# Decay matrices of the later chunks: VectorE's scans replaced by ScalarE's exponentials of cumulated logarithms, with GpSimd setting the upper triangle to zero

## The chip, the cores and the metric

One core of a Trainium2 chip runs the whole kernel. The time is the device time of one launch in microseconds (us). TensorE (PE, with its weight loads as PEld), VectorE (DVE), ScalarE (ACT), GpSimd (POOL) and SyncE (SP, which here only issues DMAs) each run their own instruction stream in order and wait for each other by semaphores.

## The reference

The first half is a state-space layer over 4 sequences, 8 heads and 768 tokens. It yields `y` per token and head; the second half is a mixture of four two-layer experts over the 3072 tokens.

```python
for c in range(nc):
    la = log_a[:, :, sl]                       # log of the decays a, clipped to 1e-6..1
    cum = np.cumsum(la, axis=-1)
    L = np.exp(cum[:, :, :, None] - cum[:, :, None, :])
    L = L * causal                             # i >= j
    M = np.einsum('bhin,bhjn->bhij', Cc, Bc) * L
    y_intra = np.einsum('bhij,bhjd->bhid', M, xc)
    y_inter = np.einsum('bhin,bhnd->bhid', Cc, state) * np.exp(cum)[:, :, :, None]
    y[:, :, sl] = y_intra + y_inter
    state = decay_full[:, :, None, None] * state + np.sum(Bx, axis=2)
...
for e in range(E):                             # x: y with the heads side by side
    out += p[:, e:e + 1] * (np.maximum(x @ w1[e], 0.0) @ w2[e])
```

`L[i, j]` is the product of the decays of the tokens j+1 to i. So a row of it can be made by a running product from a 1 on the diagonal, or as the exponential of a difference of two running sums of logarithms, with zeros where i < j.

## The kernel before

The kernel cuts each sequence into chunks of 128 tokens (not the reference's 32): 24 chunks, each with 8 heads. Chunk c belongs to sequence c mod 4, so chunks 0 to 3 are the first ones of their sequences and need no state. The chunks are grouped into five blocks of 4, 4, 4, 6 and 6, and inside a block into pairs. A block of tokens is then multiplied with the experts' weights (TensorE products at line 871, by schemes that save multiplications and pay with sums of blocks on VectorE and GpSimd: lines 898, 962, 981, 1200).

For each chunk the state-space half does this:

- `fetch` (line 741) loads the tokens `xb`, a copy `ab` of the chunk's decays to all 128 partitions (line 439, 512 KB, from the DRAM tensor `acut_d`, in which the first decay of each chunk is 0), and from the fifth chunk on `ah` (line 445, from `ac_d`, the uncut decays).
- `decays` (line 755) makes `LT`, the transposed decay matrices of the 8 heads: from chunk 3 on two VectorE scans of 128x512 (line 495), each over four heads, with the identity as addend: a running product that restarts at every diagonal. `LT` has one buffer for a pair of chunks. GpSimd's `fade` (line 505) takes the last column of `LT` for the state. For chunks from the fifth on, VectorE also scans `ah` into `dec` (line 777, 128x128), and GpSimd multiplies it into `cts` (line 780). ScalarE makes the masked `ctm` (line 471).
- `scores` (line 784): TensorE multiplies C and B for a pair (line 478) into four PSUM banks; four VectorE instructions (line 795, 128x512) multiply these with `LT` into `MT`, which has two buffers for pairs.
- `outputs` (line 803): TensorE multiplies `MT` (line 511) and the state (line 817); ScalarE copies the results out of PSUM (lines 832, 521). `carry` (line 839) updates the state on VectorE.

In the expert half the products of a unit are chained through PSUM: ScalarE copies a bank out (`snap`, line 880, and line 1148) or loads a bank with a saved partial sum (`seed`, line 885), and VectorE gates a bank with relu and probability (`gated`, line 906). TensorE's next product of the same bank waits for these copies.

The first 13 us (lines 525 to 697, chunks 0 and 1 and the start of 2) are written out by hand. All that follows is ordered at build time by `Plan` (line 81): TensorE's order is a fixed list (`line`), and for each other engine `run` (line 187) simulates the times with given durations and takes, whenever an engine is free, the ready instruction with the earliest latest permissible start (`w.latest`, line 140). Two rules of it matter here. `hold` (lines 138 and 139) tightens that start of an instruction to a given time after the product that it reads. And a free VectorE, in the first 25 us alone (`NEAR`, `FIRST`, lines 237 and 241), may leave a ready instruction and wait for a much more urgent one that is ready within 0.3 us. What comes out is a fixed instruction order on each engine and on SP's DMA queue. Where a pair's decays, scores and outputs are put into the list is said in `PAIRS_AT` (line 48).

Buffers are "homes" of a kind: 33 of kind V (128x512), 28 of kind W (weights), 8 PSUM banks, 2 `ab`, 2 `MT`, 1 `LT`.

Of the kernel before, what the change touches and what calls it, by code (L numbers as in the profile page):

```python
# [8 lines left out]
FP32 = mybir.dt.float32  # L9
AF = mybir.ActivationFunctionType  # L10
ALU = mybir.AluOpType
# [18 lines left out]
AFTER = 1  # L30
HOLD = 6.0
NEAR, WORTH, FIRST = .3, 1.0, 25.0
WAIT = .15
# [47 lines left out]
class Plan:  # L81
# [12 lines left out]
    def add(self, on, fn, reads=(), writes=(), part=(), lag=None, due=None, reuse=None, two=False,  # L94
            port=True, after=None, kb=0, hold=0.0, pieces=1):
        w = Work(on, fn, (.16 if "PE" in on else .09) if lag is None else lag)
        w.hold = hold
        w.two, w.port, w.after, w.kb, w.pieces = two, port, after, kb, pieces
        w.due, w.reuse = due, reuse
        w.ready = 0.0  # L100
        for v in reads:
            w.needs.update(v.writers)
            w.ready = max(w.ready, getattr(v, "ready", 0.0))
            v.readers.append(w)
        for v in writes:
            w.needs.update(v.writers)
            w.needs.update(v.readers)
            v.writers, v.readers = [w], []
        for v in part:
            w.needs.update(v.readers)  # L110
            v.writers = v.writers + [w]
        w.needs.discard(w)
        for v in dict.fromkeys([*reads, *writes, *part]):
            w.touched.append(v)
            v.left += 1
        for n in w.needs:
            n.feeds.append(w)
        w.number = len(self.all)
        self.all.append(w)
        return w  # L120
# [66 lines left out]
    def run(self, line, at, begin):  # L187
# [19 lines left out]
        while todo:  # L207
# [4 lines left out]
            for w in waiting[e]:  # L212
# [23 lines left out]
                else:  # L236
                    if e == "DVE" and when <= now + NEAR and now < FIRST and (near is None or rank < near[0]):
                        near = rank, when
# [103 lines left out]
def kernel(  # L342
# [33 lines left out]
    def real(c):  # L376
        return c % NSEQ * NC + c // NSEQ
# [14 lines left out]
    acut_d = tc.dram_tile([NCH, NH, P], FP32, name="acut_d")  # L392
    ac_d = tc.dram_tile([NCH, NH, P], FP32, name="ac_d")
    p_d = tc.dram_tile([E, NCH, P], FP32, name="p_d")
# [9 lines left out]
    def some(n, shape, name, pool=const):  # L404
        return [pool.tile(shape, FP32, name=f"{name}{i}") for i in range(n)]

    homes = {
        "V": some(NV, [P, 2, FB], "v"),
        "W": some(NW, [P, 2 * FB], "w"),
# [3 lines left out]
        "ah": some(3, [HN, P], "ah"),  # L413
        "LT": some(1, [P, 2, NH, P], "LT"),
        "MT": some(2, [P, 2, NH, P + N], "MT"),
# [5 lines left out]
        "gate": some(3, [P, max(b.n for b in blocks), P], "gate"),  # L421
        "Y": some(12, [P, FB], "Y"),
    }
    st = {c: {} for c in range(NCH)}
    one = nc.const_aps.tensor(1.0, [P, 1])
# [11 lines left out]

    def load_decays(c, ab):
        nc.sync.dma_start(
            out=ab, in_=acut_d[real(c)].rearrange("h s -> (h s)").partition_broadcast(P))  # L440

    def load_heads(c, ah):
        src = ac_d[real(c)].unsqueeze(1).to_broadcast([NH, N, P])
        for there, here, n in turned(c):
            nc.sync.dma_start(out=ah[here:here + n], in_=src[there // N:(there + n) // N])
# [47 lines left out]
    def scan(LT, src, lo):  # L493
# [4 lines left out]
            op0=ALU.mult, op1=ALU.add)  # L498

    def fade(c, MT, xb, LT):  # L500
        b = xb[:, OB:OB + HN].rearrange("p (h n) -> p h n", h=NH)
# [14 lines left out]
    def keep_state(c, A, y):  # L516
# [13 lines left out]
    pc = const.tile([P, NCH, E], FP32)  # L530
    a_sb, a_cut = (homes["V"][-4][:NCH * NH // 2, i].rearrange("p (r s) -> p r s", r=2) for i in range(2))
    nc.gpsimd.memset(aq0, 0.0)
# [6 lines left out]
        out=aq1.rearrange("(q r) c t s -> q r c (t s)", q=NQ)[:, 0], in_=a_rows[:, 1:SPREAD])  # L539
    warm = const.tile([P, 1], FP32)  # L540
    nc.scalar.mul(warm, one, one)

# [90 lines left out]

    LT, MT = ([homes[k][0][:, c] for c in range(2)] for k in ("LT", "MT"))
    ctm = homes["ctm"]
# [60 lines left out]
    nc.sync.dma_start(out=p_d.rearrange("e c s -> c e s"), in_=p_sb)  # L696
    store_decays(nc.sync, ac_d, a_sb)

# [38 lines left out]
    for c in range(2):  # L737
        st[c]["A"] = plan.taken("A", c, now)
    g0 = gates[0, 0] = plan.taken("gate", 0, now)

    def fetch(c):
# [5 lines left out]
        if c >= NSEQ:  # L747
            s["ah"] = value("ah")
            dma(lambda e: load_heads(c, s["ah"].t), len(turned(c)), 64,
                part=[s["ah"]])  # L750
        if "ab" not in s and c >= SPREAD:
            s["ab"] = value("ab")
            dma(lambda e: load_decays(c, s["ab"].t), 1, 512, part=[s["ab"]])

    def decays(c):
        s = st[c]
        j = c % 2
        for k in ("LT", "MT") if not j else ():
            s[k] = st[c + 1][k] = value(k)
        for part in range(2):  # L760
            if c < SPREAD:
                dve(1.2, lambda e, part=part: scan_quarters(
                    c, s["LT"].t[:, j], [b.t for b in s["a"]], part), reads=s["a"][2 * part:2 * part + 2],
                    part=[s["LT"]])
            else:
                half = NH * P // 2
                dve(1.15, lambda e, lo=half * part: scan(
                    s["LT"].t[:, j], s["ab"].t[:, lo:lo + half], place(c, lo // P) * P), two=True, reads=[s["ab"]], part=[s["LT"]])
        if c < NCH - NSEQ:
            plan.add({"POOL": .5 if place(c, 0) else .4}, lambda e: fade(c, s["MT"].t[:, j], s["xb"].t, s["LT"].t[:, j]),  # L770
                     reads=[s["xb"], s["LT"]], part=[s["MT"]])
        if "ctm" not in s:
            s["ctm"] = value("ctm")
            act(.62, lambda e: mask(c, s["ctm"].t, s["xb"].t), reads=[s["xb"]], writes=[s["ctm"]])
        if c >= NSEQ:
            s["dec"], s["cts"] = value("dec"), value("cts")
            dve(D256, lambda e: nc.vector.tensor_tensor_scan(
                out=s["dec"].t, data0=s["ah"].t, data1=zeros, initial=1.0,
                op0=ALU.mult, op1=ALU.add), two=True, reads=[s["ah"]], writes=[s["dec"]])
            plan.add({"POOL": .72}, lambda e: nc.gpsimd.tensor_mul(  # L780
# [3 lines left out]
    def scores(cs):  # L784
# [6 lines left out]
        for r in (3, 2, 0, 1):  # L791
            def fn(e, r=r):
                g = gs_[r].t.rearrange("p (c t s) -> p c t s", c=2, t=NT)[:, :len(cs)]
                js, h = slice(cs[0] % 2, cs[0] % 2 + len(cs)), quarter(cs[0], r)
                nc.vector.tensor_mul(s["MT"].t[:, js, h, 0:P], g, s["LT"].t[:, js, h])  # L795

            dve(D512 if len(cs) > 1 else D256, fn, reads=[gs_[r], s["LT"]], part=[s["MT"]], hold=HOLD)

# [104 lines left out]
    def gated(x, g, n, sign=1):  # L903
# [5 lines left out]
                [P, JJ, FB]), op0=ALU.max if sign > 0 else ALU.min, op1=ALU.mult),  # L909
            reads=[x, g], writes=[h], reuse=x, two=x.kind != "bank")  # L910
        return h
# [383 lines left out]
    twos = [(fb, fb + 1) for fb in range(0, AHEAD * EPB, 2)]  # L1295

    st[2]["a"] = [value("bank", fills=False) for _ in range(NQ)]
    fetch(3)
# [11 lines left out]
    scores([2, 3])  # L1310
    line.extend(firsts[SCORED:8])
    outputs([2, 3])
    ones = [(two, {1: begun[two][2]}) for two in twos]
    line.extend([*firsts[8:], *second(0, ones[:SOON], [(1, 2)])])
    for c in range(4):
# [148 lines left out]
```

## Time and profile before

| | us |
|---|---|
| median of 3 runs | 623.88 (623.32 to 623.90) |
| span of the profiled execution, first to last instruction | 620.9 |
| what lies around the span, if that execution took the median | 3.0 |
| PE / PEld busy | 615.4 / 526.0 |
| DVE busy | 533.5 |
| ACT busy | 275.5 |
| POOL busy | 179.1 |
| DVE scans into `LT` of 128x512 (line 495), 42 | 54.5 |
| DVE scans into `dec` (line 777), 20 | 11.7 |

The profile gives no total time of the profiled execution besides its span. Shares of busy time are averages over the whole span. A view by stretches of time gives the busy time of each engine in each stretch, with the number of instructions in brackets, then the granted TensorE clock, the DMA engines' busy share and GB/s. In the timeline, an entry has its start, how long it and the following like instructions took, the engine, line and operation, and in square brackets the idle time of the engine before it and what ended it. Matmul ends are modelled, so on TensorE the distances of the starts are the better measure.

### The profile page before, as it was taken

The numbers are of one execution on the slowest core, as the hardware profiler recorded it, in microseconds if no ns is written. First come the engines' busy times: TensorE is split into PE (matmuls) and PEld (weight loads), VectorE is DVE, ScalarE is ACT, GpSimd is POOL, SyncE is SP. The second block draws the span as 40 slices with busy tenths as digits, with TensorE's granted clock in tenths as the row PEclk, the third lists the DMA queues.
The fourth block names the chain that finished last, engine by engine and source line by source line (L and its number), as shares of the span: only waits on it lengthen the run. The fifth ranks groups of instructions, "written<-read, shape, count | busy, mean of one in ns | idle before, by whom it ended". The sixth has DMA issues, their size and how long they took to land.

```text
span 620.9 us, 10264 instructions
## 1 busy us (share of the span) xinstructions
PE 615.4 (99%) x3427; PEld 526.0 (85%) x3427; DVE 533.5 (86%) x882; ACT 275.5 (44%) x582; POOL 179.1 (29%) x205
## 2 busy tenths in 40 slices
PE   9999999999999999999999999999999999999997
PEld 5788888888888888888888888888888888888886
DVE  7999999999868779879799999959787977869684
ACT  5453373523356334235534336446443334555441
POOL 5006586544326676362542110300000000000010
PEclk9999999999999999999999999999999999999999
DMA  7997779773799779399998929635231339643001
GB/s 254 331 346 231 239 247 307 240 237 103 226 359 303 264 233 306 84 298 322 293 338 280 333 66 307 177 117 177 60 106 57 86 66 309 209 138 111 1 1 51
DMA packets 112627, 127.44 MB, mean 205 GB/s; under 512 B 28980, under 2 KB 78144, under 8 KB 112576
## 3 DMA queue, kind: packets, MB, share of 16 engines
q1 hardware_dynamic: 112420, 126.74, 63.8%
q8 instruction: 27, 0.44, 0.3%
q14 instruction: 24, 0.20, 0.1%
q10 hardware_dynamic: 156, 0.06, 0.0%
HBM read 101.87 MB, written 24.89 MB: 204 GB/s over the span
## 4 chain that ended last, share of the span: by engine, by line
PE 97%; DVE 1%; ACT 1%; issue 0%; DVEq 0%
PE bank L871 91%; PE bank L511 2%; PE bank L478 2%; PE bank L649 1%; PE bank L817 1%; PE bank L625 0%; DVE v L906 0%; DVE w L962 0%; DVE LT L495 0%; DVE MT L795 0%; ACT ctm L471 0%; DVE v L898 0%; PE bank L1269 0%; PE bank L617 0%; ACT A L521 0%
## 5 line engine op out<-in xcount | busy, mean ns | idle before, releaser
L871 PE MATMUL bank<-v,w 128*128 128x256 f32 x1816 | 429.5, 380 | 0.7 <-ACT v L880 0.3
L871 PEld LDWEIGHTS bank<-v,w 128*128 128x128 f32 x1816 | 342.7, 190 | 53.8 <-issue 4.0
L871 PE MATMUL bank<-Y,w 128*128 128x256 f32 x824 | 210.6, 379 | 0.0
L898 DVE TENSOR_TENSOR v<-v,v 128x512 f32<-128x512 f32 x258 | 188.9, 764 | 16.4 <-ACT v L880 15.2
L871 PEld LDWEIGHTS bank<-Y,w 128*128 128x128 f32 x824 | 156.3, 190 | 21.9 <-issue 0.6
L906 DVE SCALAR_TENSOR_TENSOR v<-bank,gate 128x512 f32<-128x512 f32 x172 | 116.2, 683 | 32.6 <-PE bank L871 27.7
L885 ACT COPY bank<-v 128x512 f32<-128x512 f32 (+1 forms) x201 | 112.8, 573 | 67.8 <-DVE v L898 37.1
L962 POOL TENSOR_TENSOR w<-w,w 128x256 f32<-128x256 f32 x100 | 95.1, 973 | 60.2 <-PE bank L871 23.1
L1148 ACT COPY v<-bank 128x512 f32<-128x512 f32 x106 | 62.2, 587 | 110.6 <-PE bank L871 109.7
L880 ACT COPY v<-bank 128x512 f32<-128x512 f32 x112 | 65.5, 586 | 95.7 <-PE bank L871 92.3
L898 POOL TENSOR_TENSOR v<-v,v 128x512 f32<-128x512 f32 x22 | 30.3, 1382 | 261.8 <-DVE v L898 157.6
L495 DVE TENSOR_TENSOR_SCAN LT<-ab,ident 128x512 f32<-128x512 f32 x42 | 54.5, 1317 | 0.4 <-DMA ab<-acut_d 0.4
L898 DVE TENSOR_TENSOR v<-bank,v 128x512 f32<-128x512 f32 x40 | 27.5, 687 | 7.9 <-PE bank L871 7.5
L1200 DVE TENSOR_TENSOR v<-v,v 128x256 f32<-128x256 f32 x56 | 24.6, 476 | 6.8 <-ACT v L1148 6.7
L780 POOL TENSOR_TENSOR cts<-ctm,dec 128x256 f32<-128x256 f32 x20 | 18.4, 929 | 33.3 <-ACT ctm L471 17.0
L795 DVE TENSOR_TENSOR MT<-bank,LT 128x512 f32<-128x512 f32 x44 | 27.2, 679 | 0.5
L1151 ACT COPY v<-bank 128x256 f32<-128x256 f32 x23 | 8.6, 374 | 40.2 <-PE bank L871 40.1
L505 POOL TENSOR_TENSOR MT<-xb,LT 128x64 f32<-128x64 f32 (+1 forms) x28 | 14.6, 529 | 36.9 <-DVE LT L495 29.7
L962 POOL TENSOR_TENSOR w<-w 128x256 f32<-128x256 f32 x13 | 14.6, 1125 | 20.1 <-PE bank L871 12.1
L1047 DVE TENSOR_TENSOR bank<-bank,v 128x512 f32<-128x512 f32 x24 | 16.5, 692 | 3.0 <-PE bank L871 2.8
L471 ACT ACTIVATE ctm<-xb,tmask 128x128 f32<-128x128 f32 x48 | 16.1, 397 | 0.0
L962 DVE TENSOR_TENSOR w<-w,w 128x256 f32<-128x256 f32 x38 | 16.0, 459 | 0.0
(72 smaller groups left out, 202.5 us busy)
## 6 DMA issues: line engine op xcount, KB each, us to landing
w<-w_d SPq DMA_DIRECT2D x138, 256.0 KB
w<-in_w_dram SPq DMA_DIRECT2D x126, 256.0 KB
w_d<-w SPq DMA_DIRECT2D x82, 256.0 KB
ab<-acut_d SPq DMA_DIRECT2D x21, 512.0 KB
w<-in_w_dram SPq DMA_DIRECT2D x42, 128.0 KB
gate<-p_d SPq DMA_DIRECT2D x10, 384.0 KB
xb<-in_xbc_dram SPq DMA_DIRECT2D x17, 192.0 KB
gate<-p_d SPq DMA_DIRECT2D x11, 256.0 KB
```

What stands on the lines that cost most here:

```text
L495: nc.vector.tensor_tensor_scan(out=LT.rearrange("p h s -> p (h s)")[:, lo:lo + w], data0=src, data1=ident.rearrange("p h s -> p (h s)")[:, ...
L780: plan.add({"POOL": .72}, lambda e: nc.gpsimd.tensor_mul(s["cts"].t, s["ctm"].t, s["dec"].t.unsqueeze(1).to_broadcast([HN, NT, P])), reads ...
L795: nc.vector.tensor_mul(s["MT"].t[:, js, h, 0:P], g, s["LT"].t[:, js, h])
L871: nc.tensor.matmul(out=o, lhsT=w[:, j], rhs=x if half is None else x[:, j], start=(start and j == 0), stop=(j == 1), skip_group_check=True)
L880: act(.5, lambda e: nc.scalar.copy(out=flat(v), in_=bank.t), reads=[bank], writes=[v])
L885: act(.54 if to - lo > FB else .32, lambda e: nc.scalar.copy(out=bank.t[:, lo:to], in_=flat(v)[:, lo:to]), reads=[v], writes=[bank])
L898: plan.add(engines, lambda e: (on(e).tensor_add if sign > 0 else on(e).tensor_sub)(flat(v), whole(x), whole(y)), reads=[x, y], writes=[v], ...
L906: dve(D512, lambda e: nc.vector.scalar_tensor_tensor(out=h.t, in0=whole(x).rearrange("p (j m) -> p j m", j=JJ), scalar=0.0, in1=g.t[:, 2 * ...
L962: plan.add({"POOL": .72} if due else B256, lambda e, r=r, x=x, y=y, sign=sign: (on(e).tensor_add if sign > 0 else on(e).tensor_sub)(view(r ...
L1047: dve(D512, lambda e: nc.vector.tensor_sub(b5.t, b5.t, flat(t)), reads=[t], writes=[b5])
L1148: act(.5, lambda e: nc.scalar.copy(out=flat(v), in_=bank.t), reads=[bank], writes=[v])
L1200: plan.add(engines, lambda e: (on(e).tensor_add if sign > 0 else on(e).tensor_sub)(o[1](), x[1](), y[1]()), reads=[v for v in vs if v is n ...
```

## The change

Chunks 0 to 3 keep their scans, into a tile `LT0` whose four quarters then become V homes (29 other V tiles, so again 33, and `LT` is no longer a buffer of its own). For the chunks from the fifth on:

- Once, early in the plan: ScalarE takes the logarithm of the clipped decays (128 columns of two rows, on 96 partitions), VectorE sums them up in two scans, SP stores the sums to the DRAM tensor `cum_d`, TensorE transposes them (two transposes), and ScalarE stores them negated as `neg`, one column for each chunk and head. The store of the uncut decays to `ac_d` at the end of the hand-written part goes.
- For each chunk: `ab` and `ah` are loaded from `cum_d`. Eight ScalarE exponentials of 128x128 (one for each head, the bias a column of `neg`) write straight into `MT`, two GpSimd selects of 128x512 set the part above the diagonal to zero in place, `fade` reads `MT`, one ScalarE exponential of 128x128 makes `dec`, and line 795's four products read and write `MT`.
- The planner may let ScalarE too, at any time, wait for a more urgent instruction that is ready within `NEAR`, now 0.4 us; and `gated` instructions that read a bank get a `hold` of 2 us.
- ScalarE's small warming multiplication becomes an explicit load of a table set with logarithm and exponential.

```diff
-HOLD = 6.0
-NEAR, WORTH, FIRST = .3, 1.0, 25.0
+HOLD, FREE = 6.0, 2.0
+NEAR, WORTH, FIRST = .4, 1.0, 25.0
...
+        w.needs.update(behind)
...
-                    if e == "DVE" and when <= now + NEAR and now < FIRST and (near is None or rank < near[0]):
+                    if when <= now + NEAR and (e == "ACT" or e == "DVE" and now < FIRST) and (
+                            near is None or rank < near[0]):
...
-        "V": some(NV, [P, 2, FB], "v"),
+        "V": some(NV - 4, [P, 2, FB], "v"),
...
-        "LT": some(1, [P, 2, NH, P], "LT"),
...
+        "cum": some(2, [NCH * NH // 2, 2, P], "cum"),
+        "neg": some(1, [P, 2, NCH * NH // 2], "neg"),
+        "dram": [None],
     }
+    LT0 = const.tile([P, 2, NH, P], FP32, name="LT0")
+    homes["V"][:0] = [
+        LT0[:, j, h:h + NQ].rearrange("p (a h) s -> p a (h s)", a=2)
+        for j in range(2) for h in range(0, NH, NQ)]
...
+        src = acut_d if c < NSEQ else cum_d
         nc.sync.dma_start(
-            out=ab, in_=acut_d[real(c)].rearrange("h s -> (h s)").partition_broadcast(P))
+            out=ab, in_=src[real(c)].rearrange("h s -> (h s)").partition_broadcast(P))
 
     def load_heads(c, ah):
-        src = ac_d[real(c)].unsqueeze(1).to_broadcast([NH, N, P])
+        src = cum_d[real(c)].unsqueeze(1).to_broadcast([NH, N, P])
...
+    def decay(c, MT, ab, neg, h):
+
+        nc.scalar.activation(
+            out=MT[:, place(c, h), 0:P], in_=ab[:, h * P:h * P + P], func=AF.Exp,
+            bias=neg[:, h % NT, NQ * real(c) + h // NT:NQ * real(c) + h // NT + 1])
+
+    def causal(MT, h, n):
+        nc.gpsimd.affine_select(
+            out=MT[:, h:h + n, 0:P], in_=MT[:, h:h + n, 0:P], compare_op=ALU.is_ge, fill=0.0,
+            base=0, pattern=[[0, n], [1, P]], channel_multiplier=-1)
...
-    warm = const.tile([P, 1], FP32)
-    nc.scalar.mul(warm, one, one)
+    nc.scalar.preload_act_table_set("natural_log_exp_and_others")
...
-    store_decays(nc.sync, ac_d, a_sb)
...
-        for k in ("LT", "MT") if not j else ():
-            s[k] = st[c + 1][k] = value(k)
-        for part in range(2):
-            if c < SPREAD:
-                dve(1.2, lambda e, part=part: scan_quarters(
-                    c, s["LT"].t[:, j], [b.t for b in s["a"]], part), reads=s["a"][2 * part:2 * part + 2],
-                    part=[s["LT"]])
-            else:
-                half = NH * P // 2
-                dve(1.15, lambda e, lo=half * part: scan(
-                    s["LT"].t[:, j], s["ab"].t[:, lo:lo + half], place(c, lo // P) * P), two=True, reads=[s["ab"]], part=[s["LT"]])
-        if c < NCH - NSEQ:
-            plan.add({"POOL": .5 if place(c, 0) else .4}, lambda e: fade(c, s["MT"].t[:, j], s["xb"].t, s["LT"].t[:, j]),
-                     reads=[s["xb"], s["LT"]], part=[s["MT"]])
+        if not j:
+            s["MT"] = st[c + 1]["MT"] = value("MT")
+            s["made"] = st[c + 1]["made"] = []
+        if c < NSEQ:
+            for part in range(2):
+                if c < SPREAD:
+                    dve(1.2, lambda e, part=part: scan_quarters(
+                        c, LT0[:, j], [b.t for b in s["a"]], part),
+                        reads=s["a"][2 * part:2 * part + 2], part=LTv[2 * j:2 * j + 2])
+                else:
+                    half = NH * P // 2
+                    dve(1.15, lambda e, lo=half * part: scan(
+                        LT0[:, j], s["ab"].t[:, lo:lo + half], lo), two=True,
+                        reads=[s["ab"]], part=LTv[2 * j:2 * j + 2])
+            plan.add({"POOL": .4}, lambda e: fade(
+                c, s["MT"].t[:, j], s["xb"].t, LT0[:, j]),
+                reads=[s["xb"], *LTv[2 * j:2 * j + 2]], part=[s["MT"]])
+        else:
+            made = {}
+            for h in range(NH):
+                made[h] = act(.38, lambda e, h=h: decay(
+                    c, s["MT"].t[:, j], s["ab"].t, neg.t, h),
+                    reads=[s["ab"], neg], part=[s["MT"]])
+            cut = [plan.add({"POOL": .85}, lambda e, h=h: causal(
+                s["MT"].t[:, j], place(c, h), NQ), part=[s["MT"]],
+                behind=[made[x] for x in range(h, h + NQ)]) for h in range(0, NH, NQ)]
+            s["made"] += cut
+            if c < NCH - NSEQ:
+                s["made"].append(plan.add({"POOL": .5 if place(c, 0) else .4}, lambda e: fade(
+                    c, s["MT"].t[:, j], s["xb"].t, s["MT"].t[:, j]),
+                    reads=[s["xb"]], part=[s["MT"]], behind=cut))
...
-            dve(D256, lambda e: nc.vector.tensor_tensor_scan(
-                out=s["dec"].t, data0=s["ah"].t, data1=zeros, initial=1.0,
-                op0=ALU.mult, op1=ALU.add), two=True, reads=[s["ah"]], writes=[s["dec"]])
+            act(.3, lambda e: nc.scalar.activation(out=s["dec"].t, in_=s["ah"].t, func=AF.Exp),
+                reads=[s["ah"]], writes=[s["dec"]])
...
-                nc.vector.tensor_mul(s["MT"].t[:, js, h, 0:P], g, s["LT"].t[:, js, h])
-
-            dve(D512 if len(cs) > 1 else D256, fn, reads=[gs_[r], s["LT"]], part=[s["MT"]], hold=HOLD)
+                to = s["MT"].t[:, js, h, 0:P]
+                nc.vector.tensor_mul(to, g, LT0[:, js, h] if cs[0] < NSEQ else to)
+
+            dve(D512 if len(cs) > 1 else D256, fn, reads=[gs_[r], *(LTv if cs[0] < NSEQ else ())],
+                part=[s["MT"]], hold=HOLD, behind=s["made"])
...
-            reads=[x, g], writes=[h], reuse=x, two=x.kind != "bank")
+            reads=[x, g], writes=[h], reuse=x, two=x.kind != "bank", hold=FREE if x.kind == "bank" else 0.0)
...
+    def bias():
+        turned_ = value("bank", fills=False)
+        n = NCH * NH // 2
+
+        def fn(e):
+            for r in range(2):
+                nc.tensor.transpose(turned_.t[:, r * n:r * n + n], cum.t[:, r], ident[:n, 0, :n])
+
+        pe(.3, fn, reads=[cum], writes=[turned_])
+        act(.35, lambda e: nc.scalar.mul(
+            neg.t, turned_.t[:, :2 * n].rearrange("p (r i) -> p r i", r=2), -1.0),
+            reads=[turned_], writes=[neg])
...
+    mark = line[-1]
     outputs([2, 3])
+    act(.42, lambda e: nc.scalar.activation(out=la.t, in_=la.t, func=AF.Ln), part=[la], after=mark)
+    for r in range(2):
+        dve(.6, lambda e, r=r: nc.vector.tensor_tensor_scan(
+            out=cum.t[:, r], data0=la.t[:, r], data1=zeros[:NCH * NH // 2], initial=0.0,
+            op0=ALU.add, op1=ALU.add), two=True, reads=[la], part=[cum], after=mark)
+    dma(lambda e: store_decays(nc.sync, cum_d, cum.t), kb=96, reads=[cum], part=[cd])
+
     ones = [(two, {1: begun[two][2]}) for two in twos]
-    line.extend([*firsts[8:], *second(0, ones[:SOON], [(1, 2)])])
+    rest = [*firsts[8:], *second(0, ones[:SOON], [(1, 2)])]
+    line.extend(rest[:6])
+    bias()
+    line.extend(rest[6:])
```

More of the change, by code (lines that the diff above doesn't have):

```diff
@@ L94, in add @@
     def add(self, on, fn, reads=(), writes=(), part=(), lag=None, due=None, reuse=None, two=False,
-            port=True, after=None, kb=0, hold=0.0, pieces=1):
+            port=True, after=None, kb=0, hold=0.0, pieces=1, behind=()):
         w = Work(on, fn, (.16 if "PE" in on else .09) if lag is None else lag)
@@ L392 @@
     acut_d = tc.dram_tile([NCH, NH, P], FP32, name="acut_d")
-    ac_d = tc.dram_tile([NCH, NH, P], FP32, name="ac_d")
+    cum_d = tc.dram_tile([NCH, NH, P], FP32, name="cum_d")
     p_d = tc.dram_tile([E, NCH, P], FP32, name="p_d")
@@ L530 @@
     pc = const.tile([P, NCH, E], FP32)
-    a_sb, a_cut = (homes["V"][-4][:NCH * NH // 2, i].rearrange("p (r s) -> p r s", r=2) for i in range(2))
+    a_sb = homes["cum"][0]
+    a_cut = homes["V"][-4][:NCH * NH // 2, 0].rearrange("p (r s) -> p r s", r=2)
     nc.gpsimd.memset(aq0, 0.0)
@@ L632, in scan_quarters @@
             scan(LT, banks[q][:, :NT * P], q * NT * P)
-    LT, MT = ([homes[k][0][:, c] for c in range(2)] for k in ("LT", "MT"))
+    LT, MT = ([t[:, c] for c in range(2)] for t in (LT0, homes["MT"][0]))
     ctm = homes["ctm"]
@@ L739 @@
     g0 = gates[0, 0] = plan.taken("gate", 0, now)
+    LTv = [plan.taken("V", i, now) for i in range(4)]
+    la = plan.taken("cum", 0, now)
+    cum, neg, cd = value("cum"), value("neg"), value("dram")
+    cd.dram = True
     def fetch(c):
@@ L749, in fetch @@
             dma(lambda e: load_heads(c, s["ah"].t), len(turned(c)), 64,
-                part=[s["ah"]])
+                part=[s["ah"]], reads=[cd])
         if "ab" not in s and c >= SPREAD:
             s["ab"] = value("ab")
-            dma(lambda e: load_decays(c, s["ab"].t), 1, 512, part=[s["ab"]])
+            dma(lambda e: load_decays(c, s["ab"].t), 1, 512, part=[s["ab"]],
+                reads=[cd] if c >= NSEQ else [])
     def decays(c):
```

## The prediction

> **What bounds the kernel now.** I read the page first: busy times, then the chain that ended last.
>
> ```profile
> PE 615.4 (99%) x3427; PEld 526.0 (85%) x3427; DVE 533.5 (86%) x882; ACT 275.5 (44%) x582; POOL 179.1 (29%) x205
> ...
> PE 97%; DVE 1%; ACT 1%; issue 0%; DVEq 0%
> ```
>
> TensorE carries 97% of the chain; VectorE, which the change relieves, 1%. Since matmul ends are modelled, I checked this with the starts of the matmuls of line 871 in the timeline: in calm stretches they follow each other every 0.216 us, and 2640 of them make 570 us. None of them goes. So the gain can only come from places where TensorE starts late. By stretches (busy us of each engine; brackets hold the number of instructions):
>
> ```profile
> 31.00:112.00 81.00, 80.55 (x483) 68.00 (x482) 79.16 (x126) 37.43 (x86) 46.24 (x47) 1.00 0.82 276
> 112.00:280.00 168.00, 168.00 (x1024) 144.25 (x1023) 142.43 (x217) 69.12 (x144) 86.82 (x96) 1.00 0.74 240
> 280.00:411.00 131.00, 131.00 (x719) 112.61 (x721) 119.78 (x190) 59.41 (x129) 34.54 (x36) 1.00 0.81 257
> 411.00:612.00 201.00, 201.00 (x984) 176.96 (x975) 163.31 (x281) 92.26 (x175) 2.87 (x2) 1.00 0.35 106
> ```
>
> From 112 us on TensorE never starves, at full clock (1.00). From 31 to 112 us VectorE is busy 79.16 of 81 us: there it is the tight engine, and there the late starts lie. TensorE's timeline shows them:
>
> ```profile
> 12.53 1.99 PE L871 MATMUL bank<-v,w 128*128 128x256 f32 x8
> 14.82 0.48 PE L871 MATMUL bank<-v,w 128*128 128x256 f32 x1 [0.29 <-ACT v L880]
> ...
> 57.39 1.03 PE L871 MATMUL bank<-v,w 128*128 128x256 f32 x4
> 58.66 1.56 PE L871 MATMUL bank<-v,w 128*128 128x256 f32 x6 [0.24 <-DVE v L906]
> ...
> 109.27 1.99 PE L871 MATMUL bank<-v,w 128*128 128x256 f32 x8
> 111.47 1.78 PE L871 MATMUL bank<-v,w 128*128 128x256 f32 x7 [0.21 <-DVE MT L795]
> ```
>
> Take the second pair: four matmuls from 57.39 let the next one start at 57.39 + 4 x 0.216 = 58.25; it started at 58.66, so 0.41 us was lost. The third, likewise, with 0.10 more after a switch of shapes: 111.10 against 111.47, 0.37. The first: 14.36 against 14.82, 0.46. Five smaller ones (19.6, 24.3, 25.4, 33.5, 51.3 us) sum to 0.39. At five places the second matmul after such a stop comes 0.10 late, too: 0.5. Together **2.1 us**, all that there is between 13 and 612 us. The hand-written start and the last 4 us (final transposes, output DMA) keep their work. 2.1 of 623.9 us is 0.34%; 0.2% (1.25 us) is about what a measurement of this kernel can tell from no change.
>
> **VectorE's relief.** Chunks 4 to 23 are 20. Gone are 40 scans into `LT` and 20 into `dec`:
>
> ```profile
> L495 DVE TENSOR_TENSOR_SCAN LT<-ab,ident 128x512 f32<-128x512 f32 x42 | 54.5, 1317 | 0.4 <-DMA ab<-acut_d 0.4
> ...
> L777 DVE TENSOR_TENSOR_SCAN dec<-ah,zeros 128x128 f32<-128x128 f32 x20 | 11.7, 599 | 0.0
> ```
>
> That is 40 x 1.3 + 11.7 = 64 us by busy time; two scans for the sums come, 2 x 0.4 (the shortest of line 777). Between 31 and 112 us, chunks 4 to 9 lose 12 scans and chunks 4 to 7 one of line 777 each: 79.2 - 15.6 - 2.4 = 61 of 81 us. The stops at 58 us (a gate, line 906, behind sums on VectorE) and at 111 us (the `MT` products behind a scan at 104.66 and later gates) should go, with the 0.10 after each: -0.98. Of the smaller ones with their after-stops (0.59) I take half: -0.3. The `hold` on gates only orders VectorE differently; it works in the same sense and is counted there.
>
> **ScalarE's load.** The row nearest to an exponential of 128x128 with a column as bias is the mask with a column as factor:
>
> ```profile
> L471 ACT ACTIVATE ctm<-xb,tmask 128x128 f32<-128x128 f32 x48 | 16.1, 397 | 0.0
> ```
>
> 16.1 us of union for 48 is 0.34 each (0.40 alone, a pair in 0.70). 160 + 20 exponentials at 0.35 are 63 us: 275.5 becomes 339, 55%. By stretch: 31 to 112 us, 6 chunks with 52, 37.4 + 18 = 55 of 81; 112 to 280, 8 chunks with about 72, 69 + 25 = 94 of 168; 280 to 411, 6 chunks with about 54, 59 + 19 = 78 of 131. No stretch is full, so throughput costs nothing. What may cost is order: ScalarE also feeds TensorE (lines 880, 885, 1148), and an exponential that has started ahead of such a copy delays it by up to 0.40. The cover is the planner's lookahead of 0.4 us on ScalarE; it works on simulated times. From below nothing; from above, if one exponential of each of the ten pairs hits a copy without slack, 10 x 0.35 = 3.5. I take **+0.5**, near the low end, since TensorE shows no stop at all after 112 us while ScalarE already works 40% there. The same lookahead at 13 us lets the first `snap` go before the mask of chunk 3 (13.6 instead of 14.20), but that mask then pushes the second `snap` to about 14.9: I take -0.2 of the 0.46 (bounds 0 and -0.56).
>
> The one table load in the trace takes 1.28 us (at 2.64). If copies and exponentials needed different tables, at least 40 returns of 1.28 us would come. The trace of before has no exponential, so it does not decide this. The Trainium skill ("ScalarE: Activation LUTs", Table sets) says that a set with both exp and ln exists and that cheap functions such as copy are filler in every set; by that it is the one load as before, and nothing is added.
>
> **GpSimd's selects.** 40 selects of 128x512. The only one in the trace is 128x128, 0.294 us; a copy goes from 0.295 (128 columns) to 0.393 (256), so the step per 128 columns is 0.1: 0.59 at the least, 4 x 0.294 = 1.18 at the most; I take 0.9. 36 us more on an engine that is 29% busy, off the path as long as they end before line 795. They also disturb VectorE:
>
> ```profile
> engine op xcount: duration ns min/median/max, first and last start us, forms
> ...
> L898 DVE TENSOR_TENSOR v<-v,v x258: 643/684/1757, 33.5 to 600.2; 128x512 f32<-128x512 f32 x129
> ```
>
> The usual 0.68 grows to 1.76 in the worst case. If each of 40 selects costs VectorE between 0 and 0.9, that is up to 36 us against 64 removed; the middle, 18, leaves VectorE at 533 - 63 + 18 = 488 us, still relieved. This speaks against the full gain, not for a loss. The skill has the same objection as a rule ("GPSIMD Engine Reference", Key points): GpSimd shares its SBUF interfaces with VectorE and contends with instructions that have two SBUF inputs. It gives no price; taken as total exclusion it would be the 36 us, and the stop at 111 us would partly stay.
>
> **Path of the sums.** Two transposes on TensorE: in the chain of waits four transposes of line 1269 take 0.44, so **+0.22**. They stand seven products (about 6 us) and a pair's outputs behind the mark, while logarithm (0.4) and two scans (0.8) need 1.2; VectorE is 97% busy there, but the planner ranks what TensorE waits for first. Bounds 0.2 to 1. The copy into `neg` is one 0.4 us instruction on ScalarE with 10 us in hand. SP: the store leaves 12.12 us (the loads behind it come 0.5 earlier, nothing waits for them) and is issued near 25 us; the loads of chunk 4's decays wait for its landing. Before, the store at 6.33 was waited for by SP at 10.80, 4.4 later. Chunk 4's `ab` was issued at 27.54 and its products ran at 53.7, so 4 us are covered; behind the waiting load stand stores of weight sums and loads of tokens, and the next weight loads only at 39.7. `ah` and `ab` keep their number and size. Four fewer free V homes until 21 us and the removed warming multiplication (0.30, before masks that VectorE's scans outlast) cost or bring nothing that I can see.
>
> **Sum.** -0.98 - 0.3 - 0.2 + 0.22 + 0.5 = -0.76. The span goes from 620.9 to 620.1. The profiled execution's total is not shown; with the 3.0 us between span and median unchanged: 623.88 - 0.76 = **623.1 us**.
>
> **Rivals.** (1) *All stops go and no new ones come*: 620.9 - 2.1 + 0.22 = 619.0, 622.0 with the rest; counting 0.3 of leftovers 622.3. For it: all large stops but one are VectorE's. Against: ScalarE's order changes everywhere. Faster by over 0.2% from 1.25 us on, so nearly everything has to come true. (2) *VectorE is not relieved where it matters*, as selects and sums moved by the planner take the room: the stops stay, 620.9 + 0.22 + 0.5, 624.6. (3) *Slower: the masks come late.* Before, a chunk's `ab` needed two scans (2.4 us) on one engine; now eight exponentials (2.8) and a select (0.9) on two engines that have other work: between 81.3 and 110.1 us GpSimd is busy 20.8 of 28.8 us, with sums of 0.97 us in order. Where a pair's last select ends after its scores are in PSUM, line 795 blocks VectorE, with all gates behind it, and then TensorE. Price: half a GpSimd sum, 0.5 us, at the six pairs up to 240 us beside which GpSimd is busy: 3.0, so 626.1. It decides from the point where selects end after 53.7, 74.0, 110.1, 159.8, 212.2, 240.2 us, the starts of the products before. For it: the pair at 74.0 had its last scan only 0.2 us earlier. Against: the others had 2 to 12 us.
>
> **How the numbers follow.** Forecast (623.1, between 622.6 and 624.0) 0.40; rival 1 0.28; rival 2 0.10; rival 3 with other ScalarE delays 0.22. Rivals 1 to 3 put faster by over 0.2% at 0.28, slower at 0.22, and the rest, 0.50, within. The range takes in rival 1's floor, 621.9, and most of rival 3: 621.9 to 626.0.
>
> **What would show it.** After: no line 495 after 20 us, VectorE near 61 to 67 of 81 us between 31 and 112 us, ScalarE near 55; exponentials near 0.39 us, selects near 0.9, one table load; no late matmul at 58 and 111 us. Wrong: new stops of TensorE released by lines 880, 885 or 1148 (ScalarE's order), or by line 795 after a GpSimd select (rival 3), or a wait before the transposes.

## The result and the profile after

The change made the kernel slower: 626.03 us (median of 7 runs, 625.18 to 629.25) against 623.66 (7 runs, 623.32 to 624.38), ratio 1.0050 (95% interval 1.0033 to 1.0068; the two medians alone give 1.0038). The prediction was 623.1 us, with a range from 621.9 to 626.0.

The profiled execution took 627.55 us, its span 625.8; over the seven runs the median span is 624.3 us and 1.7 us lie around it. For the kernel before, later runs give a median span of 621.5 and 2.4 us around it, not the 3.0 of the prediction. So the median span grew by 2.8 us. The profiled execution lies another 1.5 us above that median, and e9_again below shows which of its stops are larger than usual. On the page after the change, busy times and the chain that ended last:

```profile
PE 616.6 (99%) x3429; PEld 526.3 (84%) x3429; DVE 487.0 (78%) x842; ACT 328.2 (52%) x763; POOL 167.8 (27%) x227
...
PE 91%; DVE 4%; DMA 2%; ACT 2%; issue 1%; SPq 0%; DVEq 0%; ACTq 0%
```

VectorE lost 46.5 us of work, as wanted, and TensorE's share of the chain fell from 97% to 91%: the chain now leaves TensorE more often. The stretches, after the change:

```profile
31.00:112.00 81.00, 77.63 (x459) 65.48 (x458) 74.53 (x136) 54.84 (x147) 36.93 (x50) 1.00 0.89 291
112.00:280.00 168.00, 167.39 (x949) 143.63 (x948) 114.41 (x182) 88.27 (x211) 73.02 (x100) 1.00 0.74 234
280.00:411.00 131.00, 131.00 (x760) 112.63 (x759) 105.47 (x175) 74.90 (x182) 45.65 (x51) 1.00 0.80 260
```

In the first stretch TensorE now idles for 3.4 us (0.45 before), although VectorE has 4.6 us less to do there. TensorE's timeline names the places (line 913 is the former 871, 948 the gate, 927 the `seed`, 487 the scores, 1193 the former 1151, a copy out of a bank):

```profile
58.56 4.48 PE L913 MATMUL bank<-v,w 128*128 128x256 f32 x20
64.09 1.15 PE L487 MATMUL bank<-ctm,xb 32*128 32x256 f32 x16 [1.05 <-ACT v L1193]
...
87.22 1.89 PE L913 MATMUL bank<-v,w 128*128 128x256 f32 x8
90.78 1.99 PE L913 MATMUL bank<-v,w 128*128 128x256 f32 x8 [1.66 <-DVE v L948]
...
95.20 1.89 PE L913 MATMUL bank<-v,w 128*128 128x256 f32 x8
97.74 1.56 PE L913 MATMUL bank<-v,w 128*128 128x256 f32 x6 [0.65 <-ACT bank L927]
...
197.72 1.89 PE L913 MATMUL bank<-v,w 128*128 128x256 f32 x8
200.23 1.99 PE L913 MATMUL bank<-v,w 128*128 128x256 f32 x8 [0.61 <-ACT bank L927]
```

By the distances of the starts, as in the prediction (8 x 0.216 = 1.73 us after 87.22 the next matmul should start), the last three places lost 1.83, 0.82 and 0.78 us. The first lost 1.21 by the same reckoning, with the matmul records that are there. The stops at 58 and 111 us are gone, as forecast: four new ones, 4.6 us, took the place of two old ones, 0.8 us.

### The profile page after: what moved, and what is told of

Its sections match the earlier page's. It is cut to its first block, busy times and chain, and to the rows that moved or that the text cites. A ratio compares the mean times of both kernels' runs of the same rounds, so it can differ in the third digit from the quotient of the medians.

```text
span 625.8 us, 10435 instructions
## 1 busy us (share of the span) xinstructions
PE 616.6 (99%) x3429; PEld 526.3 (84%) x3429; DVE 487.0 (78%) x842; ACT 328.2 (52%) x763; POOL 167.8 (27%) x227
## 4 chain that ended last, share of the span: by engine, by line
PE 91%; DVE 4%; DMA 2%; ACT 2%; issue 1%; SPq 0%; DVEq 0%; ACTq 0%
PE bank L913 86%; PE bank L487 2%; PE bank L531 2%; DMA ab<-cum_d 1%; DVE w L1004 1%; DVE v L940 1%; DVE v L948 1%; PE bank L669 1%; PE bank L859 1%; DMA w<-in_w_dram 0%; PE bank L645 0%; ACT MT L511 0%; DVE bank L1089 0%; ACT bank L927 0%; DVE MT L836 0%
## 5 line engine op out<-in xcount | busy, mean ns | idle before, releaser
L913 PE MATMUL bank<-v,w 128*128 128x256 f32 x1572 | 376.7, 380 | 3.2 <-DVE v L948 1.7
L913 PEld LDWEIGHTS bank<-v,w 128*128 128x128 f32 x1572 | 296.6, 190 | 49.2 <-issue 2.9
L940 DVE TENSOR_TENSOR v<-v,v 128x512 f32<-128x512 f32 x187 | 132.7, 730 | 33.6 <-ACT v L922 32.4
L913 PE MATMUL bank<-LT,w 128*128 128x256 f32 x244 | 62.6, 380 | 0.0
L511 ACT ACTIVATE MT<-ab,neg 128x128 f32<-128x128 f32 x160 | 51.2, 390 | 6.1 <-DMA ab<-cum_d 3.2
L913 PEld LDWEIGHTS bank<-LT,w 128*128 128x128 f32 x244 | 46.0, 190 | 7.1 <-issue 0.7
L516 POOL TENSOR_SCALAR_AFFINE_SELECT MT<-MT 128x512 f32<-128x512 f32 x40 | 29.8, 747 | 81.3 <-ACT MT L511 76.1
L940 POOL TENSOR_TENSOR v<-v,v 128x512 f32<-128x512 f32 x4 | 6.2, 1546 | 75.7 <-DVE v L948 73.4
L836 DVE TENSOR_TENSOR MT<-bank,MT 128x512 f32<-128x512 f32 x40 | 24.8, 680 | 1.8 <-PE bank L487 1.6
L940 DVE TENSOR_TENSOR v<-v,LT 128x512 f32<-128x512 f32 x29 | 22.3, 768 | 0.6 <-PE bank L913 0.2
```

The lines of the kernel that those rows point to most:

```text
L511: nc.scalar.activation(out=MT[:, place(c, h), 0:P], in_=ab[:, h * P:h * P + P], func=AF.Exp, bias=neg[:, h % NT, NQ * real(c) + h // NT:NQ ...
L516: nc.gpsimd.affine_select(out=MT[:, h:h + n, 0:P], in_=MT[:, h:h + n, 0:P], compare_op=ALU.is_ge, fill=0.0, base=0, pattern=[[0, n], [1, P ...
L836: nc.vector.tensor_mul(to, g, LT0[:, js, h] if cs[0] < NSEQ else to)
L913: nc.tensor.matmul(out=o, lhsT=w[:, j], rhs=x if half is None else x[:, j], start=(start and j == 0), stop=(j == 1), skip_group_check=True)
L940: plan.add(engines, lambda e: (on(e).tensor_add if sign > 0 else on(e).tensor_sub)(flat(v), whole(x), whole(y)), reads=[x, y], writes=[v], ...
```

## What the stops have in common

At 97 and 200 us TensorE waits for a `seed` into a bank that a gate has just read: product, gate, `seed`, next product, all through one PSUM bank. Such a chain stops TensorE when there is no other bank for a second chain. So I asked who holds the other banks. The outputs of four chunks (line 531, at 80.7 to 82.9 us) stand in four of the eight banks until ScalarE has copied both parts out: `y` (line 874, formerly 832) and the state (line 541, formerly 521). ScalarE's timeline after the change:

```profile
81.45 0.89 ACT L874 COPY v<-bank 128x256 f32<-128x256 f32 x2 [1.09 <-PE bank L531]
82.24 1.57 ACT L511 ACTIVATE MT<-ab,neg 128x128 f32<-128x128 f32 x5
...
85.97 1.57 ACT L511 ACTIVATE MT<-ab,neg 128x128 f32<-128x128 f32 x5
...
95.07 1.57 ACT L511 ACTIVATE MT<-ab,neg 128x128 f32<-128x128 f32 x5
...
97.93 0.63 ACT L874 COPY v<-bank 128x256 f32<-128x256 f32 x2
98.58 1.49 ACT L541 COPY A<-bank 32x32 f32<-32x32 f32 x8
...
103.16 0.19 ACT L541 COPY A<-bank 128x32 f32<-128x32 f32 x1
```

The last copy of these banks starts at 103.2 us; before the change it started at 84.6. At the next outputs (176 us) it is 212.8 against 178.4. Exponentials for scores that come at 113 us run in between.

The profile does not number the banks, but the kernel's program does. The outputs at 80.7 us lie in banks 0, 1, 5 and 7; the product at 95.20 us, its gate, the `seed` at 97.10 and the product at 97.74 are all in bank 6. The stop at 88 us is a chain in bank 3: product, an add and a gate on VectorE, next product. At 197.7 us the chain that stops is in bank 5. There banks 0 and 4 still hold outputs, and two more, copied out by 194.8 us, stay empty until the scores at 216 us; the kernel before, too, leaves two banks empty from its outputs to these scores.

**Theory B (held banks).** The planner ranks ready work by its latest permissible start. The exponentials are due for the scores, the copies for the state update and the next block, which is later still; that a copy frees a bank has no price in the ranking. Before the change ScalarE ran out of more urgent work often enough for the copies to go at once. 160 exponentials fill those gaps and overtake the copies, and TensorE's chains run short of banks. **Theory S**: the selects on GpSimd come late or disturb VectorE (the prediction's third rival). **Theory D**: late DMAs of the decays block ScalarE's in-order queue. **Rival P**: the two new planner rules spoil the order by themselves.

## The experiments

**e1_hold.** Two instructions of the changed kernel get a tighter due time, nothing else.

```diff
-                out=yt.t[:, :, lo:lo + P], in_=v(y)[:, :, 0:P]), reads=[y], part=[yt])
+                out=yt.t[:, :, lo:lo + P], in_=v(y)[:, :, 0:P]), reads=[y], part=[yt], hold=HOLD)
...
-                    c, s["A"].t, v(y)[:, :, P:]), reads=[y], part=[s["A"]])
+                    c, s["A"].t, v(y)[:, :, P:]), reads=[y], part=[s["A"]], hold=HOLD)
```

> The changed kernel with one addition: ScalarE's copies of the state-space outputs out of PSUM (lines 874 and 541) get the same 6 us `hold` as the MT products, so that they go ahead of exponentials that nobody needs yet. Theory B (held banks: exponentials overtake these copies, four PSUM banks stay occupied for 16 to 20 us after the outputs at 81 and 176 us, and TensorE's chains run short of banks): the copies follow the outputs within 6 us, the stops at 88.7 (1.83), 96.7 (0.82) and 199.2 us (0.78) go, the time falls by 2.5 to 3.4 us against the changed kernel, to 622.6 to 623.5. Theory S (late selects, and GpSimd's contention with VectorE): no change beyond 0.5 us, 625.5 to 626.5. Theory D (a late DMA of the decays blocks ScalarE's queue): the stop at 62.7 us (1.2) stays, and with it the spread between runs.

Measured: 622.89 us, ratio to the kernel before 0.9984 (0.9975 to 0.9993); 3.1 us less than the changed kernel. ScalarE's timeline now has all copies in one go after the outputs, and exponentials behind them:

```profile
80.66 1.50 ACT L541 COPY A<-bank 32x32 f32<-32x32 f32 x8 [2.07 <-PE bank L531]
82.19 1.20 ACT L874 COPY v<-bank 128x256 f32<-128x256 f32 x4
83.41 0.57 ACT L541 COPY A<-bank 64x32 f32<-64x32 f32 x3
...
84.85 0.40 ACT L511 ACTIVATE MT<-ab,neg 128x128 f32<-128x128 f32 x1
```

The 24 us that begin with the outputs, first of the changed kernel, then of this one. The columns are the stretch, its length, the busy time of TensorE's matmuls, its weight loads, VectorE, ScalarE and GpSimd with the instructions of each, the granted clock, the DMA share and GB/s:

```profile
81.00:105.00 24.00, 21.68 (x151) 18.16 (x141) 22.39 (x43) 17.25 (x51) 10.07 (x15) 1.00 0.87 279
```

```profile
79.00:103.00 24.00, 24.00 (x165) 20.93 (x166) 22.95 (x49) 18.27 (x53) 9.12 (x14) 1.00 0.83 277
```

TensorE is busy throughout (21.68 us before the edit), while VectorE and ScalarE do a little more work than before it, not less. The stops at 88, 97 and 199 us are gone. Theory B's numbers came in: in the program of e1_hold, products enter two of the outputs' banks again at 85.4 and 87.2 us. The repaired kernel is 1.0 us faster than the one before, but only 0.3 of it in the span (see the last section). The stop at 62.7 us, which theory D expected to stay, is not in this profile, yet the twelve runs still spread over 2.8 us (621.5 to 624.3).

**e2_select1.** Selects of one column, order unchanged; the kernel leaves out the zeros above the diagonal.

```diff
-            out=MT[:, h:h + n, 0:P], in_=MT[:, h:h + n, 0:P], compare_op=ALU.is_ge, fill=0.0,
-            base=0, pattern=[[0, n], [1, P]], channel_multiplier=-1)
+            out=MT[:, h:h + n, 0:1], in_=MT[:, h:h + n, 0:1], compare_op=ALU.is_ge, fill=0.0,
+            base=0, pattern=[[0, n], [1, 1]], channel_multiplier=-1)
```

> The changed kernel, same order of all instructions, but each GpSimd select covers one column of each head instead of 128, so that the part above the diagonal is not set to zero (the output is another). Theory S: selects of 0.75 us become about 0.15, VectorE's two-input sums lose their neighbour, and the time falls by 1 to 3 us, to 623 to 625. Theory B: the copies out of PSUM are as late as before, and the time stays within 0.5 us of the changed kernel, 625.5 to 626.5. Theory D: also no change.

Measured: 625.03 us, ratio 1.0017 (1.0008 to 1.0025), 1.0 us less than the changed kernel: the lower edge of theory S and more than theory B allowed. But the stops at 87.1 (1.18 us), 94.5 (0.82) and 197.0 us (0.78) are all there. The selects took 0.30 us, not the 0.15 expected, and VectorE's busy time fell from 487.0 to 481.0 us. The selects add something; they do not make the stops.

**e3_late_copies.** The kernel before, no exponential, copies of chunks 4 to 11 made late by 15 us in the plan.

```diff
+        self.late = 0.0
...
-                    for n in w.needs])
+                    for n in w.needs]) + w.late
...
-                out=yt.t[:, :, lo:lo + P], in_=v(y)[:, :, 0:P]), reads=[y], part=[yt])
+                out=yt.t[:, :, lo:lo + P], in_=v(y)[:, :, 0:P]), reads=[y], part=[yt]).late = 15.0 if NSEQ <= c < 3 * NSEQ else 0.0
...
-                    c, s["A"].t, v(y)[:, :, P:]), reads=[y], part=[s["A"]])
+                    c, s["A"].t, v(y)[:, :, P:]), reads=[y], part=[s["A"]]).late = 15.0 if NSEQ <= c < 3 * NSEQ else 0.0
```

> The kernel before, without any exponential or select, but ScalarE's copies of the outputs of chunks 4 to 11 out of PSUM become ready for the planner only 15 us later. Theory B: late copies alone bring the stops back at the same places, near 89, 97 and 200 us, and cost 3 to 6 us more than the kernel before, 626.5 to 629.5. Theories S and D: no cost, within 0.5 us of the kernel before, 623.2 to 624.2.

Measured: 631.30 us, ratio 1.0126 (1.0111 to 1.0141): 7.4 us more than the kernel before, and above the 3 to 6 expected. TensorE's timeline has the stops in the same places, released by the same line (886 here):

```profile
90.44 1.13 PE L872 MATMUL bank<-v,w 128*128 128x256 f32 x4 [0.96 <-ACT bank L886]
...
97.71 2.00 PE L872 MATMUL bank<-v,w 128*128 128x256 f32 x8 [1.82 <-ACT bank L886]
...
101.29 1.13 PE L872 MATMUL bank<-v,w 128*128 128x256 f32 x4 [0.72 <-ACT bank L886]
...
204.19 2.97 PE L872 MATMUL bank<-v,w 128*128 128x256 f32 x8 [2.15 <-ACT bank L886]
```

Late copies alone are enough, without a single exponential or select. Some of the 10.4 us by which this profiled span (631.9) exceeds the usual 621.5 is another thing: from 205.0 to 208.5 us matmuls start 0.43 apart instead of 0.216, and the granted clock there is 0.51. Only this run has a mean clock of 0.997; the other three have spans near 629.2, 7.7 us above 621.5.

**e4_rules.** The kernel before with ScalarE's lookahead, `NEAR` 0.4 and the 2 us hold on gates, as in the change's diff.

> The kernel before with the two planner rules of the change alone (ScalarE's lookahead of 0.4 us, the 2 us hold on gates that read a bank). Theory B: the rules are not the cause; within 1 us of the kernel before, 622.9 to 624.7. Rival P (the changed rules spoil the order by themselves): 625 to 627, with stops after 80 us.

Measured: 624.93 us, ratio 1.0018 (1.0009 to 1.0027), 1.0 us more than the kernel before: just outside what theory B allowed (624.7), and just short of rival P's 625. Its stops are others (63.6, 234.7 and 382.7 us, 0.47 to 0.68 each).

**e8_norules.** The other way round: the change without the two rules.

> The changed kernel without the two planner rules, and without the hold on the copies out of PSUM. Theory B: exponentials overtake the copies all the same; TensorE stops near 89, 96 and 99 us, and the time stays near the changed kernel's, 625 to 627. Rival P (the rules are what spoils the order): back to the kernel before or faster, 622.5 to 624.

Measured: 627.64 us, ratio 1.0061 (1.0043 to 1.0079), not faster than the change, and a little above theory B's 625 to 627. The last copy of the first outputs starts at 96.9 us, and TensorE's timeline reads

```profile
89.92 1.13 PE L912 MATMUL bank<-v,w 128*128 128x256 f32 x4 [0.65 <-ACT bank L926]
...
96.50 1.99 PE L912 MATMUL bank<-v,w 128*128 128x256 f32 x8 [1.12 <-ACT bank L926]
...
106.17 1.13 PE L912 MATMUL bank<-Y,w 128*128 128x256 f32 x4 [1.06 <-ACT bank L926]
```

Near 200 us it has no stop. So the loss is there without the rules, and rival P falls as its cause.

**e10_defer.** The mirror of e1_hold: the copies keep their rank, the exponentials lose theirs.

```diff
+        self.defer = 0.0
...
-                rank = w.latest
+                rank = w.latest + w.defer
...
+                made[h].defer = 100.0
```

> The mirror of e1_hold: the changed kernel, no hold on the copies, but the planner ranks each of the 160 exponentials 100 us later than its due time, so that on ScalarE everything else that is ready goes first. Theory B, if the exponentials are what overtakes the copies: the copies follow the outputs within about 5 us at 80 and 175 us, the stops near 88, 97 and 199 us go, and the time is near e1_hold's, 622.5 to 624.5 (a mask that comes late near 67 us may cost up to 0.7). If the hold of e1_hold helped in another way, the stops stay: 625 to 627.

Measured: 623.86 us, ratio 0.9998 (0.9989 to 1.0007), 2.2 us less than the changed kernel. The copies (lines 876 and 542 here) again follow the outputs in ScalarE's timeline:

```profile
82.04 1.84 ACT L876 COPY v<-bank 128x256 f32<-128x256 f32 x4 [2.14 <-PE bank L532]
83.90 2.10 ACT L542 COPY A<-bank 32x32 f32<-32x32 f32 x11
```

The stops near 88, 97 and 199 us are gone, and one of 0.47 us at 66.6 is there, as the expectation allowed. From both sides, then: it is the overtaking.

**e5_hold_select1.** e1_hold with the selects of e2_select1.

> e1_hold (copies out of PSUM held to 6 us) with each GpSimd select cut to one column of each head, so that the part above the diagonal is not set to zero; the order of instructions is that of e1_hold. e2_select1 gained about 1.0 us against the changed kernel. If the selects cost by themselves (contention with VectorE, or a late mask), the same 1 us comes here: 621.4 to 622.2. If they only cost where banks are short, since a slower VectorE then reaches TensorE, nothing comes: within 0.4 us of e1_hold, 622.5 to 623.3.

Measured: 622.54 us, ratio 0.9978 (0.9967 to 0.9989), 0.35 us less than e1_hold, with intervals that overlap. With banks free, the selects' length costs nothing that these runs can tell. So the 1.0 us of e2_select1 fits what the second case expected (a slower VectorE reaches TensorE when banks are short); which of contention and late masks it was, these runs do not separate, but in the changed kernel's profile no engine waited for a select, which speaks for contention.

**e9_again.** The changed kernel, unedited.

> The changed kernel once more, for a second profile. Theory B: its order of instructions is fixed, so the stops near 88, 97 and 199 us come again, each within 0.5 us of the first profile. Theory D: the stop of 1.2 us near 62.7, which began with the landing of the decays 8 us after their issue, depends on the DMA's moment and may be gone or have another size.

Measured: one run, 625.63 us. TensorE's timeline:

```profile
88.84 1.99 PE L913 MATMUL bank<-v,w 128*128 128x256 f32 x8 [0.27 <-DVE v L948]
...
95.80 1.99 PE L913 MATMUL bank<-v,w 128*128 128x256 f32 x8 [0.65 <-ACT bank L927]
...
198.29 1.99 PE L913 MATMUL bank<-v,w 128*128 128x256 f32 x8 [0.61 <-ACT bank L927]
```

The stops of 0.82 and 0.77 us come again within 0.01; the one at 88 us is 0.43 instead of 1.83, so 1.4 us of it were that execution's, against the expectation. VectorE's timeline fits this: ahead of that product's gate, three sums of weights (line 1004) ran from 83.93 to 86.51 us, 2.58 us, beside GpSimd's sums of the same line and a select. In the second profile the same three took 1.07 us, and in e2_select1, where the stop was 1.18, they took 2.14. The stop at 62.7 us is gone, and one of 0.93 us has come at 22.9, before the outputs of chunks 2 and 3, which use no exponentials. In the first profile the stop at 62.7 us began with this entry of ScalarE's timeline,

```profile
59.74 2.45 ACT L511 ACTIVATE MT<-ab,neg 128x128 f32<-128x128 f32 x8 [2.94 <-DMA ab<-cum_d]
```

eight exponentials queued ahead of the copies that TensorE needed, waiting for decays issued at 51.73 us. In the second profile the load issued at 51.11 had landed when ScalarE came to it. So what theory D describes does occur, in single executions; it may be part of why the changed kernel's runs spread over 4.1 us (623.3 to 624.9 for the kernel before in 27 runs). The run of 628.78 us also has a mean granted clock of 0.997, which by the share alone is about 1.9 us (an estimate: 0.003 of its span). The spread was not tested further.

**e6_hold_norules and e7_hold_look.** e1_hold without the two rules, and with the lookahead alone (0.3 us, no hold on gates).

> e1_hold without the two planner rules of the change (ScalarE's lookahead, the 2 us hold on gates). The rules alone cost the kernel before about 1 us (e4_rules). If that cost is theirs, this kernel is faster than e1_hold by 0.5 to 1 us, 621.9 to 622.4; if it was an accident of that one order, within 0.5 us of e1_hold, 622.4 to 623.4.

> e1_hold with ScalarE's lookahead at 0.3 us and without the 2 us hold on gates: a try for the fastest order. Without banks held, what is left to lose is about 1 us of small stops; expected 621.8 to 622.9, with no stop of TensorE over 0.5 us after 20 us.

Measured: 622.19 us (0.9971, 0.9960 to 0.9982) and 622.24 us (0.9969, 0.9957 to 0.9981). Both beat the kernel before and lie in the expected ranges; against e1_hold the gain is 0.7 us by the medians, but the intervals overlap, so it is not shown. In e7_hold_look the largest stop after 20 us is 0.42 us, as expected. These are the fastest versions of this study: the change's idea with the copies out of PSUM held to 6 us.

## Why the prediction was wrong, point by point

- **What bounds the kernel**: right. Apart from up to 0.7 us of the start, nearly all that the profiled spans won or lost lies in late starts of TensorE between 13 and 200 us; e6_hold_norules, with TensorE busy 81.00 of 81 us there, is 1.7 us faster than the kernel before, and 2.1 us was named as the most (0.7 us of the 1.7 lies around the span, see the last section).
- **VectorE's relief**: nearly exact in total (488 us forecast, 487.0 measured), but partly by luck, and wrong in place. The 18 us put down for the selects' disturbance were 6.0 as far as e2_select1 shows; the planner also moved 19 sums from GpSimd to VectorE (lines 898 and 962: VectorE 369 before, 388 after), which the sum had not counted. For 31 to 112 us I forecast 61 to 67 us; it was 74.5. In that stretch the planner moved sums from GpSimd to VectorE: 62 VectorE instructions of lines 898 and 962 started there and took 40.4 us, each counted in full; after the change it was 81 of the same lines, and 51.4 us. The stops at 58 and 111 us went all the same.
- **ScalarE's load**: its size was nearly right (339 us forecast, 328.2 measured), and so was the row it came from:

```profile
L511 ACT ACTIVATE MT<-ab,neg 128x128 f32<-128x128 f32 x160 | 51.2, 390 | 6.1 <-DMA ab<-cum_d 3.2
...
L516 POOL TENSOR_SCALAR_AFFINE_SELECT MT<-MT 128x512 f32<-128x512 f32 x40 | 29.8, 747 | 81.3 <-ACT MT L511 76.1
```

- **The step that failed** is the next sentence there: "What may cost is order". I looked only at copies that feed TensorE directly (lines 880, 885, 1148), let an exponential delay one by at most its own 0.40 us, and took +0.5. The copies that mattered are lines 832 and 521, which feed nothing that TensorE needs soon, but free banks; whole rows of exponentials passed them, and all but the first two copies of each group came 16 to 34 us later than before. That was worth 3.1 us (e1_hold), not 0.5; with 3.1 the prediction's sum is +1.8 us, where the medians show +2.4. The sign that was named for this, new stops released by line 885 (now 927), did come, at 97 and 200 us. Even a direct delay can be more than one exponential: at 62.7 us it was a row of eight that waited for a DMA, 1.2 us in one execution. The argument for the low end, no stop after 112 us at 40% ScalarE load, was no evidence: at that load ScalarE had gaps in which the copies went at once.
- **The first stop, at 13 us**: the -0.2 did not come. The first eight products and the wait behind them took 2.27 us (13.23 to 15.50), 2.29 before.
- **Table set**: one load, 1.28 us, at 2.69 us in the changed kernel, and none at the exponentials. This agrees with what the Trainium skill ("ScalarE: Activation LUTs", Table sets) states: one set holds both exp and ln, and copy is in every set.
- **GpSimd's selects**: 0.75 us in the mean instead of 0.9; GpSimd's total fell to 167.8 us instead of rising, since the planner moved sums away. What the sharing of SBUF interfaces with VectorE (the Trainium skill, "GPSIMD Engine Reference", Key points) costs through the selects where banks are free cannot be told from zero: it is 0.35 us by the medians of e1_hold and e5_hold_select1, with overlapping intervals.
- **Path of the sums**: the two transposes took 0.17 us (29.31 to 29.48) without a wait before them; 0.22 was forecast. The store went at 28.86 us and the first load from it at 34.02, in time.
- **Rivals**: the third gave nearly the time (626.1), by luck, since the mechanism was another: line 836 waited 1.6 us in all, for TensorE's scores and not for a select, and shortening the selects left the stops. That exponentials hold back copies that only free banks was not among the cases; the upper bound of 3.5 us for ScalarE's order would have covered the 3.1, but by another mechanism.

## What to carry to other kernels

Work that is moved to a half-idle engine does not only take idle time: it fills the gaps in which that engine did, unasked, the things that have no due time of their own, such as freeing PSUM banks. Before such a move, list what the engine does that somebody waits for indirectly (buffers that it empties), and give these a due time in the schedule. And if a chain through one buffer appears in the trace (product, gate, reload of the same bank), look for who holds the other buffers, not at the chain.

## What the runs showed of the hardware that was not expected

- The time around the span was 2.4 us for the kernel before and 1.72 to 1.74 us for every kernel with the exponentials (e4_rules 2.23, e3_late_copies 2.05). It is 0.7 us of the gain of e1_hold, e6_hold_norules and e7_hold_look; the cause stays open.
- The first product of the plan started at 12.53 us in the profile before, and between 12.54 and 13.27 in the others, at 13.21 in e4_rules too, whose hand-written start is the one before. So 0.7 us of a single profile's span can be the start alone.
- In e3_late_copies the granted clock was 0.51 from 205.0 to 208.5 us, right after the longest stop of that profile (2.15 us idle before 204.19), while in the shorter stops of this and the other profiles it stayed at 1.00; why is open.
